# A causal convolution and two MLP layers on one core: staging of the weight split, order of the chains, and the crossing of block 0 changed

## The chip, the cores and the metric

One Trainium2 chip, one of its cores. The metric is the device time of one execution in microseconds; of several runs the median is given. Engines are named as the profile names them: PE (TensorE, the matmuls), PEld (its weight loads), DVE (VectorE), ACT (ScalarE), POOL (GpSimd), SP (SyncE, which here issues nearly all DMAs).

## The reference, cut to what matters

`x` is 2 x 4096 x 192, that is 8192 rows of 192 columns in fp32.

```
w   = softmax over the 7 taps of weight[8, 7]         # one set of taps for each group of 24 columns
x1  = causal convolution of x along the sequence with w
h   = x1 @ moe_w_in   (192 x 2048);  g = max(0.01 h, h);       x2  = g @ moe_w_out   (2048 x 192)
h   = x2 @ moe2_w_in  (192 x 2048);  g = h where h >= 1, 0 where h <= -1, else (h + 1)^2 / 4
out = g @ moe2_w_out  (2048 x 192)
```

## The kernel before, in words

The rows are cut into 16 blocks of 512. Columns lie on partitions. A block's layer is a **chain** of 8 **pairs**; a pair takes 256 of the 2048 hidden columns in two halves, e = 0 and 1. A pair's **up** (`add_up`, L594) makes two banks of hidden values from 18 matmuls, and its **down** (`add_down`, L657) adds them into the block's result. The pairs are numbered n = 0 to 255 in the order of the list `pairs` (L799 to L810), so U4 is the up of pair 4 and D4 its down. Since inputs and weights are fp32, each is split into a high part in the matmul's type (fp32r) and a low rest, and products high x high, high x low and low x high are added. The ups and the late downs use half the rows of the array for each of two matmuls that run side by side.

Pairs 0 to 15 (EARLY, L804) are layer one of blocks 0 and 1, interleaved; from then on a chain follows a chain in the order of `chains` (L805): before, block 2 of layer one (pairs 16 to 23), blocks 0 and 1 of layer two (24 to 39), block 3 of layer one (40 to 47), block 2 of layer two, and so on, alternating. A layer-two chain needs all 8 pieces of that layer's weights the first time; both layers' weights then stay on the chip. PE's order is `steps` (L812 to L817): U(n+2) stands ahead of D(n).

Between up and down a pair's values pass three engines. In layer one ACT applies the leaky function twice (`gh` and the bank itself, L625), and DVE subtracts (`gl`, L630). In layer two DVE clips (`s`, L638), ACT squares (L643), DVE takes the maximum (`g`, L647), ACT rounds it (`gh`, L650) and POOL subtracts (`gl`, L653).

**The weights** come in 32 pieces, 16 a layer, an in piece and an out piece for each p (`add_weights`, L229). The DRAM words are 8 bytes (`raw` has a low word and a high word). The steps of a piece: load by SP (L241 or L249); `lower` on ACT (L257) scales the high word into `ba`; `shift` on DVE (L261) moves its bits; `sign` on DVE (L264) sets the sign; `rest` on DVE (L270) scales the low word into `bp`; `total` on POOL (L274) adds both; `copy` on ACT (L285) makes the high part; `sub` on POOL (L290) the low part. `shift` and `sign` write a tile of their own, `wf`.

**The convolution** of a block (`add_conv`, L433 on): blocks 0 and 1 are transposed by PE (L486), take some of their taps on PE (L537, L542) and the others on DVE (L531); blocks 2 and up are transposed by DVE (L521) and have 12 taps on DVE. The result is split by `add_split` (ACT L406, then DVE or, for block 0, POOL, L410). The matmuls that take columns 64 to 127 and 0 to 63 from the other half of the partitions need `add_cross`: for block 0 two copies on ACT (L427) and two subtractions on DVE (L432), for all others two DMAs from the tile to itself (L420).

**The order of the work** is made on the host when the program is built. Every step is added to a `Plan` (L36) with its engine, a cost in ns, what it reads and writes, and, for PE's main steps, a due time. `Plan.order` (L79) computes the latest time of each step and then lists steps: an engine that is free takes the ready step with the earliest latest time. `COUNT` (L194) gives the buffers of each tile. On the chip each engine runs its list strictly in order.

Of the kernel before, what the change touches and what calls it, by code (L numbers as in the profile page):

```python
# [145 lines left out]
def kernel(  # L146
# [267 lines left out]
    def add_cross(dst, y=None):  # L414

        halves = (slice(0, DB), slice(DB, 128)), (slice(DB, 128), slice(0, DB))
        for to, of in halves:
            if y is None:
                plan.add(
                    dma, 300, lambda to=to, of=of: nc.sync.dma_start(  # L420
                        out=dst()[to, 2:4].bitcast(F32), in_=dst()[of, 0:2].bitcast(F32)
                    ),
                    reads=[(dst, 0), (dst, 1)], writes=[(dst, 2), (dst, 3)], uses=[dst],
                )
                continue
            plan.add(
                act, 610, lambda to=to, of=of: nc.scalar.copy(dst()[to, 2], y()[of]),  # L427
                reads=[y], writes=[(dst, 2)], uses=[dst],
            )
            plan.add(  # L430
                dve, 710,
                lambda to=to, of=of: nc.vector.tensor_tensor(  # L432
                    out=dst()[to, 3], in0=y()[of], in1=dst()[of, 0], op=ALU.subtract  # L433
                ),
                reads=[y, (dst, 0)], writes=[(dst, 3)], uses=[dst],
            )

    def add_conv(at, j):
# [33 lines left out]
        if early:  # L472
# [31 lines left out]
        else:  # L504
# [40 lines left out]
        for i in range(2):  # L545
            y = ys[i]
            if early and i:
                for k in range(NP):
# [4 lines left out]
            else:
# [314 lines left out]
```

## Time and profile before

| | |
|---|---|
| median of 3 runs | 1156.53 us (1156.28 to 1156.88) |
| the profiled execution, its own time | 1156.47 us |
| its span, first to last instruction | 1154.8 us |
| PE busy | 1137.4 us, 99% of the span |
| DVE busy | 865.3 us, 75% |
| ACT busy | 752.1 us, 65% |
| POOL busy | 421.6 us, 37% |
| TensorE clock granted, mean | 0.997 |

The page gives shares of the whole span. The program has three stages with different loads: the start up to pair 2, where blocks 0 and 1 are convolved and the first weights are made; the stretch in which weights are still being made; and the long rest with all weights there. So the windows and lines below are cut by stage. A busy PE is counted from a matmul's start to a modelled end, so short waits are seen better in the times between starts and in the waits that the timeline prints in brackets.

### The profile page before, as it was taken

How to read it: one execution, taken by the hardware profiler on the slowest of the kernel's cores; microseconds unless marked ns; L12 is line 12 of the kernel's file. 1: busy time of each engine (PE TensorE's matmuls, PEld its weight loads, DVE VectorE, ACT ScalarE, POOL GpSimd, SP SyncE). 2: the span in 40 equal slices, each digit the busy share in tenths (PEclk: the TensorE clock that was granted, in tenths of full speed). 3: DMA queues.
4: the chain of work that ended last, by engine and by line, in shares of the span. 5: the costliest groups of instructions: out<-in, count | busy, mean ns of one | idle time of the engine just before them, and what ended most of it. 6: DMA issues, size and time to landing. Idle time of an engine off the chain costs nothing.

```text
span 1154.8 us, 24741 instructions
## 1 busy us (share of the span) xinstructions
PE 1137.4 (99%) x9662; PEld 1081.5 (94%) x9662; DVE 865.3 (75%) x1278; ACT 752.1 (65%) x1320; POOL 421.6 (37%) x375
## 2 busy tenths in 40 slices
PE   8999979999999999999999999999999999999998
PEld 4778957888999999999999999999999999999998
DVE  7899989968678685877858678685867866474774
ACT  5767766656576675757667576665757666575764
POOL 4544587315051240604225061331605224060354
PEclk9999999999999999999999999999999999999999
DMA  4625122202002020110202002020210100000000
GB/s 129 158 71 143 56 60 51 52 1 56 15 19 52 19 47 6 39 32 19 51 8 50 15 20 51 20 49 4 46 25 20 33 20 20 15 20 15 20 12 17
DMA packets 124484, 44.87 MB, mean 39 GB/s; under 512 B 108624, under 2 KB 120400, under 8 KB 124368
## 3 DMA queue, kind: packets, MB, share of 16 engines
q1 hardware_dynamic: 123952, 43.08, 16.8%
q8 instruction: 75, 1.23, 0.4%
q14 instruction: 41, 0.34, 0.1%
q10 hardware_dynamic: 416, 0.23, 0.1%
HBM read 20.74 MB, written 6.29 MB: 23 GB/s over the span
## 4 chain that ended last, share of the span: by engine, by line
PE 95%; DVE 2%; issue 1%; ACT 1%; POOL 1%; DMA 1%; SPq 0%; ACTq 0%; DVEq 0%; POOLq 0%
PE bank L590 90%; PE bank L675 3%; PE bank L537 1%; DMA wraw<-in_x_dram 1%; DVE g L647 0%; DVE wf L261 0%; DVE s L638 0%; PE bank L763 0%; ACT s L643 0%; POOL wa L274 0%; DVE wp L270 0%; PE bank L542 0%; POOL gl L653 0%; PE bank L312 0%; ACT wa L257 0%
## 5 line engine op out<-in xcount | busy, mean ns | idle before, releaser
L590 PE MATMUL bank<-x,wi_h 64*128 64x512 f32 x3072 | 533.5, 388 | 4.1 <-ACT wi_h L285 2.7
L653 POOL TENSOR_TENSOR gl<-g,gh 128x512 fp32r<-128x512 f32 x256 | 339.6, 1347 | 497.5 <-ACT gh L650 491.7
L590 PEld LDWEIGHTS bank<-x,wi_h 64*128 64x128 f32 x3072 | 403.5, 184 | 21.2 <-issue 4.1
L590 PE MATMUL bank<-x,wi_l 64*128 64x512 f32 x1536 | 392.7, 387 | 2.1 <-POOL wi_l L290 2.1
L625 ACT ACTIVATE gh<-bank 128x512 fp32r<-128x512 f32 x246 | 146.4, 599 | 199.2 <-PE bank L590 194.4
L630 DVE TENSOR_TENSOR gl<-bank,gh 128x512 fp32r<-128x512 f32 x246 | 165.1, 681 | 147.8 <-PE bank L590 111.3
L590 PE MATMUL bank<-gh,wo_b 64*128 64x512 f32 x960 | 249.5, 388 | 1.9 <-POOL wo_b L290 1.9
L590 PE MATMUL bank<-gl,wo_b 64*128 64x512 f32 x960 | 249.5, 388 | 0.0
L590 PE MATMUL bank<-gh,wo_h 64*128 64x512 f32 x960 | 249.2, 387 | 0.0
L590 PE MATMUL bank<-gh,wo_l 64*128 64x512 f32 x960 | 249.0, 387 | 0.0
L590 PE MATMUL bank<-gl,wo_h 64*128 64x512 f32 x960 | 249.0, 387 | 0.0
L590 PEld LDWEIGHTS bank<-x,wi_l 64*128 64x128 f32 x1536 | 236.5, 184 | 8.5 <-POOL wi_l L290 3.0
L643 ACT ACTIVATE s<-s,half 128x512 f32<-128x512 f32 x256 | 173.4, 718 | 105.1 <-DVE s L638 103.6
L638 DVE TENSOR_SCALAR s<-bank 128x512 f32<-128x512 f32 x256 | 164.9, 684 | 83.0 <-PE bank L590 82.4
L647 DVE TENSOR_TENSOR g<-bank,s 128x512 f32<-128x512 f32 x256 | 168.5, 686 | 28.9 <-ACT s L643 22.9
L650 ACT CAST gh<-g 128x512 fp32r<-128x512 f32 x256 | 156.2, 619 | 43.4 <-DVE g L647 38.3
L590 PEld LDWEIGHTS bank<-gh,wo_b 64*128 64x128 f32 x960 | 152.1, 185 | 4.6 <-POOL wo_b L290 2.3
L590 PEld LDWEIGHTS bank<-gl,wo_b 64*128 64x128 f32 x960 | 151.7, 185 | 3.0 <-POOL gl L653 0.8
L590 PEld LDWEIGHTS bank<-gh,wo_h 64*128 64x128 f32 x960 | 152.0, 185 | 2.2
L590 PEld LDWEIGHTS bank<-gh,wo_l 64*128 64x128 f32 x960 | 151.9, 185 | 2.3
L590 PEld LDWEIGHTS bank<-gl,wo_h 64*128 64x128 f32 x960 | 151.8, 185 | 2.3
L531 DVE SCALAR_TENSOR_TENSOR xy<-xT,taps,xy 128x512 f32<-128x512 f32 x171 | 150.6, 911 | 0.6
(120 smaller groups left out, 790.2 us busy)
## 6 DMA issues: line engine op xcount, KB each, us to landing
x<-x SPq DMA_DIRECT2D x62, 256.0 KB, 3.6
xy<-in_x_dram SPq DMA_DIRECT2D x112, 64.0 KB, 2.5
wraw<-in_moe_w_in_dram SPq DMA_DIRECT2D x32, 192.0 KB, 3.4
wraw<-in_moe_w_out_dram SPq DMA_DIRECT2D x16, 384.0 KB, 3.2
out_dram<-o SPq DMA_DIRECT2D x90, 64.0 KB, 1.9
wraw<-in_x_dram SPq DMA_DIRECT2D x2, 384.0 KB, 6.1
out_dram<-s SPq DMA_DIRECT2D x1, 192.0 KB, 2.0
out_dram<-s ACTq DMA_DIRECT2D x1, 192.0 KB, 2.0
```

The costliest lines, as they stand in the source:

```text
L531: nc.vector.scalar_tensor_tensor(out=ys[i](), in0=t()[:, i, k:k + T], scalar=taps[:, i, k:k + 1], in1=ys[i](), op0=ALU.mult, op1=ALU.add,)
L537: nc.tensor.matmul(out=ys[1](), lhsT=flat(k), rhs=t()[:, 1, 2 * k:2 * k + T], start=(k == 0), stop=(k == NP - 1))
L590: nc.tensor.matmul(out=out_(), lhsT=w[e][r], rhs=v[e][r], start=start and i == 0, stop=stop and i == len(todo) - 1)
L625: lambda dst=dst, h=h: nc.scalar.activation(out=dst(), in_=h(), func=ACTF.Prelu, alpha=0.01),
L630: lambda a=a, b=b, h=h: nc.vector.tensor_tensor(out=b(), in0=h(), in1=a(), op=ALU.subtract),
L638: lambda s=s, h=h: nc.vector.tensor_scalar(s(), h(), 1.0, -1.0, ALU.min, ALU.max),
L643: lambda s=s: nc.scalar.activation(out=s(), in_=s(), func=ACTF.Square, scale=0.5, bias=half),
L647: dve, 680, lambda s=s, g=g, h=h: nc.vector.tensor_tensor(out=g(), in0=h(), in1=s(), op=ALU.max),
L650: plan.add(act, 620, lambda a=a, g=g: nc.scalar.copy(a(), g()), reads=[g], writes=[a])
L653: lambda a=a, b=b, g=g: nc.gpsimd.tensor_tensor(out=b(), in0=g(), in1=a(), op=ALU.subtract),
L675: nc.tensor.matmul(out=out_[part](), lhsT=w, rhs=v, start=start and i == 0, stop=stop and i == len(todo) - 1)
```

## The change

Four parts. (1) `wf` is gone: `shift` and `sign` work in place in `ba`, of which there are four (`wa=4`, two before), and `wp` has three. (2) `rest` runs on POOL instead of DVE, 32 times. (3) The chains go block 2 of layer one, blocks 0, 1 **and 2** of layer two, blocks 3 and 4 of layer one, and from there alternating as before; the loads of x for blocks 3 and up are not planned before the up of a pair 16 pairs earlier. (4) Block 0 is crossed by two DMAs as the others are. Besides, the convolutions of blocks 0 and 1 are added at steps of their own (`C0`, `C1`), so that four of PE's taps for block 1 stand in one run in PE's list, and the planner's costs are set anew.

```
-    COUNT = dict(wraw=4, wf=2, wa=2, wp=2, xy=4, ...)
+    LEAD = 16
+    COUNT = dict(wraw=4, wa=4, wp=3, xy=4, ...)
...
+        bits = lambda: ba().bitcast(U32)
         def shift():
-            nc.vector.tensor_scalar(bf(), ba().bitcast(U32), 3, None, ALU.logical_shift_left)
+            nc.vector.tensor_scalar(bits(), bits(), 3, None, ALU.logical_shift_left)
         def sign():
             nc.vector.scalar_tensor_tensor(
-                out=bf(), in0=raw()[:, :, 1], scalar=0x80000000, in1=bf(), op0=ALU.bitwise_and, op1=ALU.bitwise_or
+                out=bits(), in0=raw()[:, :, 1], scalar=0x80000000, in1=bits(), op0=ALU.bitwise_and, op1=ALU.bitwise_or
             )
         def rest():
-            nc.vector.tensor_scalar(bp(), raw()[:, :, 0], 2.0 ** -29, None, ALU.mult)
+            nc.gpsimd.tensor_scalar(bp(), raw()[:, :, 0], 2.0 ** -29, None, ALU.mult)
...
-        plan.add(act, 550, lower, reads=[raw], writes=[ba])
-        plan.add(dve, 430, rest, reads=[raw], writes=[bp])
-        plan.add(dve, 400, shift, reads=[ba], writes=[bf])
-        plan.add(dve, 600, sign, reads=[raw, bf], writes=[bf])
-        plan.add(pool, 1220, total, reads=[bf, bp], writes=[ba])
+        plan.add(act, 555, lower, reads=[raw], writes=[ba])
+        plan.add(pool, 800, rest, reads=[raw], writes=[bp])
+        plan.add(dve, 470, shift, reads=[ba], writes=[ba])
+        plan.add(dve, 715, sign, reads=[raw, ba], writes=[ba], chain=ba)
+        plan.add(pool, 1110, total, reads=[ba, bp], writes=[ba], chain=ba)
...
             if i == 0:
-                add_cross(dst, None if j else y)
+                add_cross(dst)
...
-                plan.add(dma, 2300, lambda i=i: load(i), reads=["under way"], writes=[raws[i]])
+                plan.add(dma, 2300, lambda i=i: load(i), reads=[("under way", at // 2 - LEAD)] if at // 2 > LEAD else ["under way"], writes=[raws[i]])
...
-    chains = [(0, 2), (1, 0), (1, 1)]
-    for j in range(3, NB):
+    chains = [(0, 2), (1, 0), (1, 1), (1, 2), (0, 3)]
+    for j in range(4, NB):
         chains += [(0, j), (1, j - 1)]
...
-    steps = ["U0", "U1", "D0"]
+    steps = ["C0", "U0", "U1", "C1", "D0"]
```

What it moves, at three places. On POOL, around the first `gl` of pair 24, the first pair of layer two (`wp` is the scaled low word, `wa` the whole word, the names with 85, 89 and 91 are layer two's split weights). Before:

```order
L274 TENSOR_TENSOR wa<-wf,wp 128x384
L460 COPY xT<-xT 128x2x6
L290 TENSOR_TENSOR wo_l_89<-wa,wo_h_87 128x256
L290 TENSOR_TENSOR wo_b_91<-wa,wo_b_91 128x2x64
L653 TENSOR_TENSOR gl<-g,gh 128x512 x2
L274 TENSOR_TENSOR wa<-wf,wp 128x384
L653 TENSOR_TENSOR gl<-g,gh 128x512 x2
L290 TENSOR_TENSOR wi_l_85<-wa,wi_h_83 128x384
```

After:

```order
L292 TENSOR_TENSOR wi_l_85<-wa,wi_h_83 128x384
L272 TENSOR_SCALAR wp<-wraw 128x384 x2
L292 TENSOR_TENSOR wo_b_91<-wa,wo_b_91 128x2x64
L642 TENSOR_TENSOR gl<-g,gh 128x512 x2
L276 TENSOR_TENSOR wa<-wa,wp 128x384
L292 TENSOR_TENSOR wo_l_89<-wa,wo_h_87 128x256
L642 TENSOR_TENSOR gl<-g,gh 128x512 x2
L292 TENSOR_TENSOR wi_l_85<-wa,wi_h_83 128x384
```

Ahead of the first `gl` stand before 24 totals, 12 `wi_l`, 12 `wo_l` and 12 `wo_b`; after, 32 scalings, 29 totals, 15 `wi_l`, 13 `wo_l` and 14 `wo_b`. So all scalings, and all but the end of the last three pieces, now come before layer two.

On DVE, from the last maximum of pair 28 to the first of pair 30 (`s` clips, `g` maxima of layer two, `wp`, `wf` weight steps). Before:

```order
L647 TENSOR_TENSOR g<-bank_65,s 128x512
L638 TENSOR_SCALAR s<-bank_66 128x512
L638 TENSOR_SCALAR s<-bank_67 128x512
L270 TENSOR_SCALAR wp<-wraw 128x384 x2
L261 TENSOR_SCALAR wf<-wa 128x384 x2
L264 SCALAR_TENSOR_TENSOR wf<-wraw,wf 128x384
L647 TENSOR_TENSOR g<-bank_66,s 128x512
L647 TENSOR_TENSOR g<-bank_67,s 128x512
L638 TENSOR_SCALAR s<-bank_64 128x512
L638 TENSOR_SCALAR s<-bank_65 128x512
L264 SCALAR_TENSOR_TENSOR wf<-wraw,wf 128x384
L647 TENSOR_TENSOR g<-bank_64,s 128x512
```

After:

```order
L636 TENSOR_TENSOR g<-bank_65,s 128x512
L627 TENSOR_SCALAR s<-bank_66 128x512
L627 TENSOR_SCALAR s<-bank_67 128x512
L412 TENSOR_TENSOR x<-yz,x 128x512
L636 TENSOR_TENSOR g<-bank_66,s 128x512
L636 TENSOR_TENSOR g<-bank_67,s 128x512
L510 STREAM_TRANSPOSE xT<-xy 128x512
L627 TENSOR_SCALAR s<-bank_64 128x512
L627 TENSOR_SCALAR s<-bank_65 128x512
L510 STREAM_TRANSPOSE xT<-xy 128x512
L636 TENSOR_TENSOR g<-bank_64,s 128x512
```

The weight steps have left this place. From the end of pair 15's values to the end of pair 31's there are 117 DVE instructions before (14 `wp`, 15 + 14 `wf`, 12 taps, 3 transposes) and 86 after (none of `wp`, 12 shifts, 13 signs, 2 taps, 2 transposes); the clips, maxima and subtractions of the pairs are the same 48 but for one clip.

On SP, early in the program, with block 0's crossing (`x<-x`). Before:

```order
L249 DMA wraw<-in_moe_w_in_dram 64x3x256 x2
L241 DMA wraw<-in_moe_w_out_dram 128x2x384
L249 DMA wraw<-in_moe_w_in_dram 64x3x256 x2
L241 DMA wraw<-in_moe_w_out_dram 128x2x384
L249 DMA wraw<-in_moe_w_in_dram 64x3x256 x2
L420 DMA x<-x 64x1024 x2
```

After:

```order
L251 DMA wraw<-in_moe_w_in_dram 64x3x256 x2
L243 DMA wraw<-in_moe_w_out_dram 128x2x384
L421 DMA x<-x 64x1024 x2
L251 DMA wraw<-in_moe_w_in_dram 64x3x256 x2
L243 DMA wraw<-in_moe_w_out_dram 128x2x384
L251 DMA wraw<-in_moe_w_in_dram 64x3x256 x2
L421 DMA x<-x 64x1024 x2
```

The first `x<-x` after is block 0's, ahead of the loads of pieces p = 2; the second, like the only one before, is block 1's.

## Rows read from the trace of the kernel before

**Rows 1.** The page: busy us, share of the span, instructions.

```profile
PE 1137.4 (99%) x9662; PEld 1081.5 (94%) x9662; DVE 865.3 (75%) x1278; ACT 752.1 (65%) x1320; POOL 421.6 (37%) x375
```

**Rows 2.** Windows: from:to, length, busy (count) of PE PEld DVE ACT POOL, PEclk, DMA.

```profile
102.78:150.57 47.79, 47.79 (x419) 46.59 (x419) 46.41 (x73) 36.72 (x72) 26.30 (x26) 1.00 0.28 79
150.57:185.36 34.79, 26.64 (x189) 19.44 (x188) 31.35 (x46) 22.00 (x42) 30.03 (x28) 0.90 0.26 58
185.36:1147.00 961.64, 961.64 (x8483) 944.98 (x8479) 699.84 (x1009) 622.99 (x1061) 316.45 (x251) 1.00 0.13 27
94.40:177.53 83.13, 76.90 (x624) 67.73 (x622) 77.47 (x118) 58.82 (x115) 53.88 (x53) 0.98 0.28 75
```

**Rows 3.** Timeline of PE, 144 to 170 us: start, length, and wait before.

```profile
144.78 0.48 PE L590 MATMUL bank<-gh,wo_b 64*128 64x512 f32 x2
...
149.09 0.47 PE L590 MATMUL bank<-gh,wo_b 64*128 64x512 f32 x2
...
159.00 0.73 PE L590 MATMUL bank<-x,wi_h 64*128 64x512 f32 x4 [2.02 <-ACT wi_h L285]
...
169.09 0.50 PE L590 MATMUL bank<-x,wi_l 64*128 64x512 f32 x2 [1.49 <-POOL wi_l L290]
```

**Rows 4.** Lines of DVE, 94.45 to 177.5 us: count, busy us, mean ns, idle before.

```profile
L270 DVE TENSOR_SCALAR wp<-wraw 128x384 uint32<-128x384 uint32 x14 | 11.7, 856 | 0.0
L638 DVE TENSOR_SCALAR s<-bank 128x512 f32<-128x512 f32 x17 | 11.1, 681 | 1.2 <-PE bank L590 1.1
L531 DVE SCALAR_TENSOR_TENSOR xy<-xT,taps,xy 128x512 f32<-128x512 f32 x12 | 10.7, 890 | 0.1
L264 DVE SCALAR_TENSOR_TENSOR wf<-wraw,wf 128x384 uint32<-128x384 uint32 x15 | 8.5, 581 | 0.2
L261 DVE TENSOR_SCALAR wf<-wa 128x384 uint32<-128x384 uint32 x15 | 8.4, 576 | 1.2 <-ACT wa L257 1.1
L410 DVE TENSOR_TENSOR x<-yz,x 128x512 fp32r<-128x512 f32 x4 | 4.1, 1027 | 0.1
```

**Rows 5.** Lines of POOL, 5 to 200 us, same columns.

```profile
L274 POOL TENSOR_TENSOR wa<-wf,wp 128x384 uint32<-128x384 uint32 x32 | 35.5, 1111 | 57.2 <-DVE wf L264 41.4 <-DVE wp L270 8.7 <-ACT xy L527 6.5
L290 POOL TENSOR_TENSOR wi_l<-wa,wi_h 128x384 fp32r<-128x384 f32 x16 | 18.0, 1127 | 5.9 <-ACT wi_h L285 5.9
L290 POOL TENSOR_TENSOR wo_l<-wa,wo_h 128x256 fp32r<-128x256 f32 x16 | 13.8, 861 | 0.7 <-ACT wo_h L285 0.7
L290 POOL TENSOR_TENSOR wo_b<-wa,wo_b 128x128 fp32r<-128x128 f32 x16 | 8.8, 553 | 8.1 <-ACT wo_b L285 8.1
```

**Rows 6.** Timelines of POOL and of DVE, the first 26 us.

```profile
2.56 0.29 POOL masks.py:199 TENSOR_SCALAR_AFFINE_SELECT ident<-ident 128x128 f32<-128x128 f32 x1
...
15.47 1.27 POOL L410 TENSOR_TENSOR x<-xy,x 128x512 fp32r<-128x512 f32 x1 [2.08 <-ACT x L406]
17.96 1.18 POOL L274 TENSOR_TENSOR wa<-wf,wp 128x384 uint32<-128x384 uint32 x1 [1.22 <-DVE wf L264]
...
18.20 1.16 DVE L270 TENSOR_SCALAR wp<-wraw 128x384 uint32<-128x384 uint32 x1
...
25.27 0.36 DVE L270 TENSOR_SCALAR wp<-wraw 128x384 uint32<-128x384 uint32 x1
```

**Rows 7.** The chain that ended last, up to 60 us: start, length, what.

```profile
18.68 0.90 PE bank L590 x6
...
41.30 4.33 PE bank L590 x36
45.63 4.78 PE bank L675 x20
```

**Rows 8.** Block 1's crossing: SP's timeline, and line L420 to 130 us.

```profile
27.12 1.17 SPq L420 DMA_DIRECT2D x<-x  x2
...
DMA to landing us min/median/max: 3.1/4.0/4.7
```

**Rows 9.** Page, costliest groups: ACT's step on a layer-one pair's values.

```profile
L625 ACT ACTIVATE gh<-bank 128x512 fp32r<-128x512 f32 x246 | 146.4, 599 | 199.2 <-PE bank L590 194.4
```

More of the change, by code (lines that the diff above doesn't have):

```diff
@@ L294, in add_weights @@
         if o == 0:
-            copy(550, wi_h[m][:, g], ba)
-            sub(pool, 1280, wi_l[m][:, g], ba, wi_h[m][:, g])
+            copy(510, wi_h[m][:, g], ba)
+            sub(pool, 1130, wi_l[m][:, g], ba, wi_h[m][:, g])
         else:
@@ L300, in add_weights @@
             copy(300, wo_b[m][:, k, 0, :], lambda: v()[:, :, 128:D], 1)
-            sub(pool, 1020, wo_l[m][:, k, :], lambda: v()[:, :, 0:128], wo_h[m][:, k, :])
-            sub(pool, 670, wo_b[m][:, k, 1, :], lambda: v()[:, :, 128:D], wo_b[m][:, k, 0, :], 1)
+            sub(pool, 860, wo_l[m][:, k, :], lambda: v()[:, :, 0:128], wo_h[m][:, k, :])
+            sub(pool, 550, wo_b[m][:, k, 1, :], lambda: v()[:, :, 128:D], wo_b[m][:, k, 0, :], 1)
     def add_warm():
@@ L412, in add_split, with add_cross @@
         )
[L414 to L425, printed above, removed]
-            plan.add(
[L427 to L433, printed above, removed]
+    def add_cross(dst):
+        for to, of in (slice(0, DB), slice(DB, 128)), (slice(DB, 128), slice(0, DB)):
+            plan.add(
+                dma, 300,
+                lambda to=to, of=of: nc.sync.dma_start(
+                    out=dst()[to, 2:4].bitcast(F32), in_=dst()[of, 0:2].bitcast(F32)
                 ),
-                reads=[y, (dst, 0)], writes=[(dst, 3)], uses=[dst],
+                reads=[(dst, 0), (dst, 1)], writes=[(dst, 2), (dst, 3)], uses=[dst],
             )
@@ L475, in add_conv @@
             plan.add(
-                dma, 1000,
+                dma, 800 if j else 3400,
                 lambda: nc.sync.dma_start(out=v(), in_=x[b, s0:s0 + T, :].rearrange("(n p) c -> p n c", p=128)),
@@ L550, in add_conv @@
                         pe, 870, lambda k=k: tap_pair(k), reads=[("diagonal", k), (t, 1)], writes=[y],
-                        uses=[t, spare], chain=(y, "taps"),
+                        uses=[t, spare], chain="main" if j else (y, "taps"),
                     )
@@ L564, in add_conv @@
                     plan.add(
-                        dve, 780, lambda i=i, k=k: tap(i, k), reads=[(t, i), y], writes=[y], uses=[t],
+                        dve, 900, lambda i=i, k=k: tap(i, k), reads=[(t, i), y], writes=[y], uses=[t],
                         chain=(y, "taps"),
@@ L609, in add_up @@
                 pe, 3 * PASS, lambda c=c: up(c), reads=[(src, 2 * c), (src, 2 * c + 1), (("w", m, 0, p), 0)],
-                writes=[*hs] + (["under way"] if n == GO else []), uses=[src], due=main(3 * PASS), chain="main",
+                writes=[*hs] + [("under way", n)] + (["under way"] if n == GO else []), uses=[src], due=main(3 * PASS), chain="main",
             )
@@ L825 @@
             up, n = step[0] == "U", int(step[1:])
+            if step[0] == "C":
+                add_conv(2 * pairs.index((0, n, 0)) - AHEAD, n)
+                continue
             m, j, p = pairs[n]
-            if up and m == p == 0:
+            if up and m == p == 0 and j >= E0:
                 add_conv(2 * n - AHEAD, j)
```

8 lines of the change are left out of this document (4 added, 4 removed).

## The prediction

> **What bounds the kernel now.** I read the page first: PE is busy 99% of the span [rows 1], which alone says that only the remaining waits can go. Then the windows [rows 2]. From 185.36 us on PE is busy in all 961.64 us, so nothing there can be won by moving other engines' work. From 102.78 to 150.57 it is busy too. Between, from 150.57 to 185.36, it is busy for 26.64 of 34.79 us, and the granted clock is 0.90. That stretch is layer two of block 0, while the weights of layer two are still being made.
>
> Then PE's timeline, for the waits themselves [rows 3]. Without waits the same matmul of two pairs in a row starts at 144.78 and at 149.09, so a pair takes 4.31 us. The bracketed waits name POOL (`wi_l`) and ACT (`wi_h`): PE waits for weights. But the engine named is only the last in a row. Who is late is seen in the window from 94.40 to 177.53, which runs from the last DVE instruction on pair 15's values to the last on pair 31's: DVE is busy 77.47 of 83.13 us, while POOL is busy 53.88 and ACT 58.82 [rows 2]. Sixteen pairs need 16 x 4.31 = 69.0 us of PE; they took 83.1. So **DVE is the bound there, and costs PE 14.1 us**. Its lines say what it does [rows 4]: beside the pairs' own values, 14 scalings of low words at 0.856 us (11.7 us busy), 30 shifts and signs (16.9 us), and 12 convolution taps for block 3 (10.7 us).
>
> The second place is the start. The chain of waits has the first up at 18.68 us and U4 at 41.30 [rows 7]. From U4 on the chain is PE alone, 4.33 us for two ups and 4.78 us for two downs [rows 7], to the end of the first stage.
>
> **The change part by part.**
>
> *DVE from pair 16 to 31.* By the changed order it has 86 instructions where 117 were. At the measured means [rows 4]: 48 clips, maxima and subtractions x 0.681 = 32.7; 12 shifts x 0.576 = 6.9; 13 signs x 0.581 = 7.6; 2 taps x 0.890 = 1.8; 11 others at no more than 1.027 = 11.3. Sum 60.3 us against 69.0 us of PE: DVE now has 8.7 us to spare where it was 14.1 short. (A sum of means is an upper figure, since neighbouring records overlap at their ends: the 17 clips, 11.6 us by their mean, are 11.1 us busy [rows 4].) What went: the scalings (to POOL), ten taps (to the two later layer-two chains), and five weight steps (done earlier). So the wait of the stretch goes: **14.1 us**, less if DVE's order still makes PE wait (the first rival).
>
> *Where the moved taps stand.* By the changed order DVE has, in the three layer-two chains (pairs 24 to 47), 96 clips and maxima, 21 taps (block 3's and nine of block 4's), 6 weight steps and 20 others: 65.4 + 18.7 + 3.5 and 20 at 0.681 to 1.027, together 101.2 to 108.1 us by means, 4% less for the overlap: 97 to 104. PE takes 24 x 4.31 = 103.4. So the cover is thin here: DVE nearly sets the pace for 100 us, though it comes to the stretch with time to spare and may be a pair late before PE waits. Bounds 0 and 4 us of new waits; I take **0.5**, nearer the lower end, since the pairs that follow one layer-two chain ran without waits at a like density of taps (from 185.36 us on [rows 2]).
>
> *The scaling on POOL.* No row shows a GpSimd multiply of 128 x 384 32-bit words. From below: a one-input POOL operation on 128 x 128 took 0.29 us [rows 6], three times that is 0.87, an upper figure if part of 0.29 is fixed. From above: the two-input add on the same 128 x 384 takes 1.11 us [rows 5]. I take 0.8, and keep 0.3 and 1.1 as bounds from these rows; a slower conversion is the second rival. POOL then has, ahead of the first `gl` of layer two, 32 scalings x 0.8 + 29 totals x 1.111 + 15 `wi_l` x 1.127 + 13 `wo_l` x 0.861 + 14 `wo_b` x 0.553 = 25.6 + 32.2 + 16.9 + 11.2 + 7.7 = 93.6 us, plus some 4 us for block 0's low part (1.27 [rows 6]) and small copies: about 98. It can start at about 8 us, and the pairs of layer two begin at 102.78 + 6 x 4.31, some 128 us: 22 us to spare. In the first stage two downs and two ups take 9.1 us [rows 7], and a pair of pieces costs POOL 1.6 + 2.2 + 1.1 + 0.9 + 0.6 = 6.4. So POOL's added 25.6 us cost nothing at the end; the cover is the 22 us.
>
> *In-place shift and sign, more `wa` tiles.* Same instructions, no time of their own: the four tiles let a piece start before the last one's `sub` is through.
>
> *Block 0 crossed by DMA.* Two copies of ACT and two subtractions of DVE go; two DMAs come, issued by SP in 1.17 us, and they landed 3.1 to 4.7 us after their issue for block 1 [rows 8]. They wait for block 0's low part on POOL, which ended at 15.47 + 1.27 = 16.7 us before [rows 6]. After, the three DVE taps ahead of it start about 1 us sooner (the first piece's shift and sign now stand behind them), but those two (1.16) stand ahead of the add: 15.2 to 16.7. With 0.6 us to the second issue and 3.1 to 4.7 to land, U0's last third starts at 19.0 to 22.1; I take 20.1. SP queues the loads of p = 2 behind the crossing; they come 1.2 us later and are needed only by U2. The gain of the two ACT and two DVE steps is in this chain, not beside it.
>
> *From there to U4.* U0 ends at 20.1 + 0.8 = 20.9. On ACT stand `gh`, a `lower`, three more leaky steps, then block 1's high part: six at about 0.6 [rows 9], to 24.5; on DVE then block 1's low part and the first `gl`, 2 x 0.68: 25.8. U1 and the four taps of block 1 (now in one run) are done on PE by then. D0 is half of 2.4 us behind each of two `gl`: ends at 28.2. Then two ups 4.33 and two downs 4.78 [rows 7]: U4 at 37.3 instead of 41.30. Weights do not stop it: POOL, walked the same way, has p = 2's `wo_b` at 34.7 for D2 at 34.9. **Gain 4.0 us**, with 5.1 and 2.0 at the ends of the crossing, and 1 if POOL is a little later.
>
> *The clock.* PE now stands idle for about 2.5 us ahead of U0 and 2.3 us in it. Before, waits such as 2.02 and 1.49 us, 8.15 us in all, went with a granted clock of 0.90 over 34.79 us [rows 2, 3], that is 3.5 us lost. Half as much waiting in the start may cost half of it, 1.7, or nothing, as before; I take 0.8.
>
> **The sum**, against the profiled execution's own 1156.47 us (0.06 below the median; its span is 1.67 less): 1156.47 - 14.1 + 0.5 - 4.0 + 0.8 = **1139.7 us**.
>
> **The rivals.**
>
> *The stretch keeps part of its wait, by the port.* A DVE scaling took 0.36 us alone and 1.16 us beside a POOL add [rows 6], which itself took 1.18 instead of some 1.0; its mean was 0.856 [rows 4]. So DVE and POOL hold each other up, and 25.6 us more of POOL can hold DVE. If each of the 16 layer-two scalings holds a DVE step by its 0.8, that is 12.8 us against 8.7 to spare: 4.1 back. If DVE's idle time in the stretch (83.13 - 77.47 = 5.7 us [rows 2]) comes again, 9.8 back. So 1144 to 1149.5. Against it: the scalings that did the waiting are themselves gone from DVE, and clips, maxima and subtractions, which read a bank, stay at 0.68 beside a busy POOL. The Trainium skill, page "SBUF — State Buffer", section "Who interferes with whom", says that GpSimd shares a port pair with VectorE as an exclusive lock, so that one of the two fully blocks for a whole instruction. By that rule this rival is what moving work to GpSimd does; rows 6 agree with it.
>
> *POOL becomes the bound* (slower). POOL's place is ahead of the first `gl` of layer two. If a scaling takes r, POOL is late by 32 x (r - 0.8) - 22 us, and PE waits there instead. That eats the gain of 16.8 at r = 2.0 us; at 2.5 it is 1139.7 + 54.4 - 22 = 1172. For it: it multiplies whole numbers by a fraction and reads every second word, which no POOL row of before does. Against it: the add of two inputs is 1.11 on the same size [rows 5].
>
> *The order does not carry it:* the list is made by costs, and if block 0's crossing, loads and conversions come in another rhythm, start and stretch each keep most of their waits: 1150 to 1157.
>
> **How the numbers follow.** Forecast 0.76, port 0.16, POOL 0.05, order 0.03. A measurement of this kernel can tell about 0.2%, 2.3 us. Faster: all but POOL's and half of the last, 0.93; slower 0.05; the same 0.02. The range runs from the best start with no wait left, 1156.47 - 14.1 - 5.1 = 1137.3, rounded to 1137.0, into the port's rival to 1147.0.
>
> **What would show it.** Right: U4 at 36 to 39 us; no bracketed PE wait over 0.5 us from 100 us to the end; a granted clock of 1.00 from 40 us to 1130; DVE busy under 60 us over pairs 16 to 31; `rest` on POOL at 0.7 to 1.1 us. Wrong: PE waits on POOL `gl` or `wi_l` past 120 us, DVE shifts or taps over 1.0 us on the mean, or U0's last third after 22 us.

## The result, and the profile after

The changed kernel takes **1139.97 us** (median of 4 runs, 1139.70 to 1140.33), the kernel before 1156.70 beside it (median of 4): a ratio of 0.9852, 95% interval 0.9835 to 0.9869. Forecast were 1139.7 us, in a range of 1137.0 to 1147.0. The span of the profiled execution went from 1154.8 to 1138.3 us.

The page's first part, as [rows 1]:

```profile
PE 1130.9 (99%) x9662; PEld 950.2 (83%) x9662; DVE 862.9 (76%) x1244; ACT 752.1 (66%) x1318; POOL 466.2 (41%) x407
```

PE's share reads 99% before and after. What changed stands in the windows (columns as in [rows 2]):

```profile
100.51:1130.66 1030.15, 1030.15 (x9085) 879.13 (x9085) 780.89 (x1112) 681.57 (x1170) 385.39 (x310) 1.00 0.15 31
91.87:162.57 70.70, 70.70 (x602) 57.60 (x603) 56.00 (x88) 55.81 (x110) 65.56 (x63) 1.00 0.35 87
126.42:229.96 103.54, 103.54 (x914) 86.94 (x912) 98.09 (x142) 74.75 (x125) 77.50 (x65) 1.00 0.16 32
```

The first row begins at U18, the up of the third pair of block 2 in layer one, six pairs ahead of layer two: from there to the last down PE waits for nothing, at a granted clock of 1.00 (by the starts of its ups 0.3 us in all are lost there). The second row is the stretch from the last DVE step on pair 15 to the last on pair 31: 70.70 us, where it was 83.13 with DVE busy 77.47 of them [rows 2]. (It is cut at DVE's steps, so the 12.4 us between the two are not PE's gain; that is read from PE's own starts below.) DVE is now busy 56.00, and POOL, at 65.56 of 70.70, is the fuller engine. The third row is the three chains in a row (pairs 24 to 47): DVE is busy 95% of it, and PE still waits for nothing.

The chain that ended last, as [rows 7] (start, length, what):

```profile
36.41 2.56 PE bank L664 x10
38.97 4.33 PE bank L579 x36
43.30 4.78 PE bank L664 x20
...
100.51 1030.15 PE bank L579 x9084
```

U4 starts at 38.97 us instead of 41.30. By its first matmul, U18 starts at 100.44 instead of 102.71, and the last down of layer two at 1130.27 instead of 1146.62. So the 16.5 us of span split in two, but for 0.1 behind the last down: **2.3 us up to U18, and 14.1 us behind it** (1043.91 us from U18 to that last down before, 1029.83 after).

Steps of DVE and POOL, 5 to 200 us (line, count, busy us, mean ns, idle before), as [rows 5]; the first line is the taps, the others are weight steps. (The layers' weights lie in DRAM as 64-bit floats, not as fp32; these steps make one fp32 word of the two 32-bit halves.) In the kernel before, the same 5 to 200 us had 0.946 us on the mean for a tap, 0.701 for a sign and 0.495 for a shift; [rows 4] has a shorter window:

```profile
L520 DVE SCALAR_TENSOR_TENSOR xy<-xT,taps,xy 128x512 f32<-128x512 f32 x27 | 27.6, 1035 | 0.2
L266 DVE SCALAR_TENSOR_TENSOR wa<-wraw,wa 128x384 uint32<-128x384 uint32 x32 | 24.0, 753 | 0.8
L263 DVE TENSOR_SCALAR wa<-wa 128x384 uint32<-128x384 uint32 x32 | 20.2, 632 | 3.4 <-ACT wa L259 3.3
```

```profile
L272 POOL TENSOR_SCALAR wp<-wraw 128x384 uint32<-128x384 uint32 x32 | 41.4, 1295 | 8.6 <-DMA wraw<-in_moe_w_in_dram 5.7 <-DMA wraw<-in_moe_w_out_dram 0.5
L276 POOL TENSOR_TENSOR wa<-wa,wp 128x384 uint32<-128x384 uint32 x32 | 34.2, 1072 | 9.3 <-DVE wa L266 8.4
```

A scaling on POOL takes 1.295 us, not the 0.8 that was taken, and more than the add of two inputs on the same tile.

### The profile page after: what moved, and what is told of

It is laid out like the page before. It is cut to its first block, busy times and chain, and to the rows that moved or that the text cites. A ratio compares the mean times of both kernels' runs of the same rounds, so it can differ in the third digit from the quotient of the medians.

```text
span 1138.3 us, 24723 instructions
## 1 busy us (share of the span) xinstructions
PE 1130.9 (99%) x9662; PEld 950.2 (83%) x9662; DVE 862.9 (76%) x1244; ACT 752.1 (66%) x1318; POOL 466.2 (41%) x407
## 4 chain that ended last, share of the span: by engine, by line
PE 96%; POOL 1%; DVE 1%; DMA 1%; issue 0%; ACT 0%; SPq 0%; DVEq 0%; POOLq 0%; ACTq 0%
PE bank L579 93%; PE bank L664 3%; POOL wp L272 0%; DMA wraw<-in_moe_w_in_dram 0%; DMA raw_taps<-in_weight_dram 0%; POOL wa L276 0%; PE bank L752 0%; DVE wa L263 0%; DVE xy L520 0%; DVE x L389 0%; POOL wi_l L292 0%; POOL wo_b L292 0%; DVE xy L559 0%; DVE wa L266 0%; ACT wi_h L287 0%
## 5 line engine op out<-in xcount | busy, mean ns | idle before, releaser
L579 PE MATMUL bank<-x,wi_l 64*128 64x512 f32 x1536 | 441.5, 386 | 0.0
L579 PEld LDWEIGHTS bank<-x,wi_l 64*128 64x128 f32 x1536 | 264.4, 184 | 25.9
L579 PE MATMUL bank<-gh,wo_h 64*128 64x512 f32 x960 | 282.5, 386 | 0.0
L579 PE MATMUL bank<-gh,wo_b 64*128 64x512 f32 x960 | 282.5, 386 | 0.0
L579 PE MATMUL bank<-gh,wo_l 64*128 64x512 f32 x960 | 282.5, 386 | 0.0
L579 PE MATMUL bank<-gl,wo_b 64*128 64x512 f32 x960 | 282.5, 386 | 0.0
L579 PE MATMUL bank<-gl,wo_h 64*128 64x512 f32 x960 | 282.3, 386 | 0.0
L579 PEld LDWEIGHTS bank<-gh,wo_h 64*128 64x128 f32 x960 | 170.8, 184 | 16.1 <-DVE yz L685 0.3
L579 PEld LDWEIGHTS bank<-gl,wo_h 64*128 64x128 f32 x960 | 170.8, 184 | 15.9
L520 DVE SCALAR_TENSOR_TENSOR xy<-xT,taps,xy 128x512 f32<-128x512 f32 x171 | 171.8, 1022 | 0.6
```

Source lines behind the costliest of these rows:

```text
L520: nc.vector.scalar_tensor_tensor(out=ys[i](), in0=t()[:, i, k:k + T], scalar=taps[:, i, k:k + 1], in1=ys[i](), op0=ALU.mult, op1=ALU.add,)
L579: nc.tensor.matmul(out=out_(), lhsT=w[e][r], rhs=v[e][r], start=start and i == 0, stop=stop and i == len(todo) - 1)
```

## The experiments

Twelve kernels. The change has four parts: the **scaling** on POOL, the staging **tiles** (shift and sign in place, four `wa`, three `wp`), the three **chains** in a row, and the **crossing** of block 0 by DMA. The first four runs undo one part each in the changed kernel, three others make one part alone in the kernel before, and the rest vary one size or put single scalings back. The crossing alone was not run, and no run undoes what goes with the four parts by itself: the planner's other costs, the later loads of x, and the steps `C0` and `C1`. In the table, times are medians, the other columns are from one profiled execution each: U4 the start of its first matmul in us, "U18" that start against the changed kernel's 100.44 us, "behind" the time from U18 to the last down of layer two, over its 1029.83, and "ahead" how many of the 32 pieces POOL has started to add before it starts its first `gl` of layer two. The profiled execution of a_wa2 was the fastest of its eleven, 1155.35 us. One profile's start is good to some 0.6 us: U0 began between 16.67 and 17.30 us in the changed kernel and those that differ from it by one part or size (a_rest2 left out).

| Kernel | us | U4 | U18 | behind | ahead |
|---|---|---|---|---|---|
| before | 1156.5 | 41.23 | +2.3 | +14.1 | 24 |
| changed | 1140.0 | 38.90 | 0 | 0 | 29 |
| u_rest: scaling undone | 1142.8 | 38.49 | -0.5 | +2.4 | 29 |
| u_chains: chains undone | 1142.7 | 39.74 | +0.9 | +1.7 | 29 |
| u_cross: crossing undone | 1142.9 | 38.89 | +1.2 | +1.3 | 29 |
| u_tiles: tiles undone | 1159.3 | 42.75 | +3.8 | +16.5 | 25 |
| b_rest: scaling alone | 1156.7 | 39.98 | +1.0 | +15.5 | 25 |
| b_tiles: tiles alone | 1147.5 | 39.71 | +0.8 | +6.3 | 27 |
| b_chains: chains alone | 1160.4 | 41.62 | +2.7 | +16.3 | 24 |
| a_wa2: two `wa` tiles | 1158.1 | 41.70 | +2.7 | +12.6 | 25 |
| a_wp2: two `wp` tiles | 1143.4 | 41.14 | +2.4 | +1.4 | 29 |

### One part undone: u_rest, u_chains, u_cross, u_tiles

u_rest:

```diff
-            nc.gpsimd.tensor_scalar(bp(), raw()[:, :, 0], 2.0 ** -29, None, ALU.mult)
+            nc.vector.tensor_scalar(bp(), raw()[:, :, 0], 2.0 ** -29, None, ALU.mult)
-        plan.add(pool, 800, rest, reads=[raw], writes=[bp])
+        plan.add(dve, 430, rest, reads=[raw], writes=[bp])
```

> The changed kernel with the scaling of the low words back on DVE (its planner cost 430), all else as changed. Load theory (what DVE has to do from pair 16 to 31 against PE's 68.9 us decides): DVE gets 14 scalings back there but still has only 1 tap, by its means 68.8 us, and its worst lateness over any row of pairs is 5.3 us, where the kernel before had 19.1 us and lost 14.1: 0 to 1.5 us of waits, 1140 to 1142 us, most of it in the start. Rival 'the scaling alone is the cause': the 14 scalings are half of what left DVE there, so at least 7 us come back, 1147 us or more, with waits of PE between 130 and 180 us. Rival 'port': with less work on POOL, taps fall from 1.02 to about 0.95 us and shifts from 0.63 to 0.5.

Measured 1142.82 us (1141.92 to 1143.49), ratio 0.988 (0.9865 to 0.9895), 0.8 us over the load theory's range. The scaling is not the cause of the gain: with all 32 back on DVE, 13.6 of the 16.5 us stay. The price is 2.4 us behind U18, and PE has it in one place, between the starts of U34 and U35 at the end of layer two's first block. The timeline brackets 1.4 us of it as waits (start, length, and in brackets the wait before):

```profile
171.89 0.50 PE L579 MATMUL bank<-gh,wo_b 64*128 64x512 f32 x1 [0.25 <-ACT yz L683]
173.53 0.50 PE L579 MATMUL bank<-gh,wo_b 64*128 64x512 f32 x1 [1.14 <-DVE yz L685]
```

The port rival missed: taps stayed at 1.043 us (shifts fell to 0.526, signs rose to 0.903).

u_chains:

```diff
-    chains = [(0, 2), (1, 0), (1, 1), (1, 2), (0, 3)]
-    for j in range(4, NB):
+    chains = [(0, 2), (1, 0), (1, 1)]
+    for j in range(3, NB):
```

> The changed kernel with the old order of the chains of layer two (two in a row instead of three), all else as changed. Load theory: 9 taps of block 3 come back into pairs 16 to 31, 64.4 us of DVE by its means against 68.9 of PE, worst lateness 3.8 us: no wait, 1140 to 1141 us. Rival 'the order of the chains is the cause': the ten moved taps (10.7 of the 22.4 us that left DVE) bring back half of the gain or more, 1147 us or more, with waits of PE between 130 and 185 us.

Measured 1142.67 us (1141.75 to 1142.92), ratio 0.9877 (0.9861 to 0.9894): 1.7 us over the load theory's end and far from the rival's. The order of the chains isn't the cause either. The 1.7 us behind U18 are lost between 136 and 155 us, where PE's waits of 0.17 to 0.33 us (at 138, 146 and 151 us) name DVE. The nine taps that stand between U16 and U33 are not shown as their cause: two of them run at 122 and 123 us, and the other seven from 151 us on.

u_cross puts the two ACT copies and the two DVE subtractions of the kernel before back for block 0:

```diff
-                add_cross(dst)
+                add_cross(dst, None if j else y)
```

> The changed kernel with block 0 crossed by two ACT copies and two DVE subtractions again, all else as changed. Load theory for the stretch: nothing of it changes, no PE wait past 100 us. Start: the two DMAs land at 19.05 and 20.28 us in the changed kernel, and U4 starts at 38.97; with the two ACT and two DVE steps back, 2.6 us of those engines stand in the chain again, as in the kernel before (U4 at 41.30): U4 at 39.5 to 41.3, 1140.5 to 1142.3 us. Rival 'the start's gain is the two convolution runs and the order, not the crossing': U4 within 0.4 us of 38.97, 1139.6 to 1140.4 us.

Measured 1142.90 us (1142.74 to 1143.00), ratio 0.9881 (0.9867 to 0.9896): over both ranges. U4 starts at 38.89 us, as in the changed kernel: **the crossing by DMA gains nothing at the place where the prediction put its gain.** U2 even starts 0.7 us earlier (28.48 against 29.22), and then waits for POOL:

```profile
30.22 0.50 PE L592 MATMUL bank<-x,wi_l 64*128 64x512 f32 x2 [1.00 <-POOL wi_l L292]
```

The 2.9 us come later: 1.2 by U18, with two waits of 0.5 and 0.1 us in the first stage, at 74 and 75 us; 0.7 at U34, with a wait of 0.25 at 173; and 0.7 between 236 and 245 us. The list that the planner makes with these four steps in it is another one; what in it makes these waits was not followed up.

u_tiles has the old tiles, and shift and sign write another tile:

```diff
-    COUNT = dict(wraw=4, wa=4, wp=3, xy=4, xT=2, x=3, yz=3, g=2, s=2, gh=4, gl=4, o=1)
+    COUNT = dict(wraw=4, wf=2, wa=2, wp=2, xy=4, xT=2, x=3, yz=3, g=2, s=2, gh=4, gl=4, o=1)
...
-            nc.vector.tensor_scalar(bits(), bits(), 3, None, ALU.logical_shift_left)
+            nc.vector.tensor_scalar(bf(), bits(), 3, None, ALU.logical_shift_left)
```

> The changed kernel with the old staging tiles (two for the words, two for the bits, two for the rest; shift and sign write another tile), all else as changed. Load theory with a lead: a piece then waits for the subtraction of the piece before the last, so fewer weight steps are done ahead of the layer-two chain; DVE has 64.7 us by its means in pairs 16 to 31 but 111.8 in pairs 23 to 47 against 103.4 of PE, worst lateness 11.0 us (26 to 42), of which some 5 were free in the kernel before: 4 to 7 us of waits between 130 and 210 us, 1144 to 1147 us. Rival 'tiles cost nothing, the load of pairs 16 to 31 alone decides': 1140 to 1141 us.

Measured **1159.34 us** (1157.17 to 1161.73), ratio 1.0026 (1.0016 to 1.0035): slower than the kernel before, and 12 us over the higher of the two expectations. Three parts of the change together, without the tiles, are worth less than nothing. PE's waits (line, waited for, total, times, longest) name another engine than before:

```profile
PE bank L579 <- POOL gl L642: 4.2, 2, 2.7
PE bank L579 <- POOL wo_b L292: 2.8, 1, 2.8
PE bank L664 <- POOL wo_b L292: 1.5, 1, 1.5
PE bank L579 <- POOL wi_l L292: 1.2, 1, 1.2
```

The window from 150 to 190 us, of the kernel before, of u_tiles and then of the changed kernel:

```profile
150.00:190.00 40.00, 31.85 (x236) 23.84 (x234) 36.56 (x54) 25.83 (x48) 33.47 (x30) 0.91 0.23 50
```

```profile
150.00:190.00 40.00, 31.26 (x209) 23.40 (x207) 34.23 (x46) 20.93 (x39) 39.16 (x35) 0.83 0.24 46
```

```profile
150.00:190.00 40.00, 40.00 (x353) 33.27 (x351) 38.87 (x56) 27.71 (x47) 28.71 (x25) 1.00 0.15 23
```

POOL is busy 39.16 of 40 us and is the bound. The theory counted DVE's load alone; it fell here. In its place: **how far the conversion of the weights runs ahead of layer two decides, and the tiles set that.** The table's last two columns say it over all its kernels: with 24 or 25 pieces ahead they lose 12.6 to 16.5 us behind U18, with 27 they lose 6.3, with 29 at most 2.4. (a_rest2, below, is the exception, with 29 ahead and 13.7 lost: there POOL's work itself is made longer.) POOL's groups up to 131 us, shortly before it starts its first `gl` of layer two (at 131.4 to 137.1 us), count the pieces that have come to the add (of 32). u_tiles, then b_tiles (below), then the changed kernel:

```profile
L276 POOL TENSOR_TENSOR wa<-wf,wp 128x384 uint32<-128x384 uint32 x25 | 26.4, 1064 | 24.4 <-DVE wf L266 23.4 <-ACT xT L487 0.6
```

```profile
L275 POOL TENSOR_TENSOR wa<-wa,wp 128x384 uint32<-128x384 uint32 x27 | 29.3, 1084 | 43.1 <-DVE wp L271 29.4 <-DVE wa L265 13.6
```

```profile
L276 POOL TENSOR_TENSOR wa<-wa,wp 128x384 uint32<-128x384 uint32 x29 | 30.7, 1062 | 9.3 <-DVE wa L266 8.4
```

The kernel before has 24. What is missing at 131 us is done in the same 60 us in which POOL has the `gl` of layer two.

### One part alone: b_rest, b_tiles, b_chains

b_rest makes only u_rest's edit the other way round, in the kernel before.

> The kernel before with the scaling of the low words on POOL alone (planner cost 800), old staging tiles, old chains, old crossing. POOL theory, formed on the run with the old tiles (there POOL was busy 39.2 of the 40 us from 150 to 190, PE waited for its gl, wo_b and wi_l, and the run came out 2.8 us slower than before): with two tiles of each kind POOL can't work ahead in the first stage, its scalings fall into the stretch of layer two, and POOL takes DVE's place as the bound: 1156 to 1165 us, PE's waits there name POOL, POOL busy over 18.5 of 20 us from 150 to 170 and from 170 to 190. DVE-load theory, as it stood before the runs: DVE falls from 82.5 to 72.2 us in pairs 16 to 31, worst lateness 8.9 us, some 5 of them free: 1145 to 1148 us.

Measured 1156.69 us (1156.07 to 1157.04), ratio 0.9996 (0.9987 to 1.0006): no difference. In the window from 150 to 190 us DVE falls to 31.98 us of work (36.56 in the kernel before) and POOL rises to 36.71 (33.47), 18.67 of it up to 170 us and 18.04 behind, where the POOL theory wanted over 18.5 in both:

```profile
150.00:190.00 40.00, 31.10 (x229) 23.17 (x227) 31.98 (x46) 25.04 (x47) 36.71 (x32) 0.91 0.18 37
```

PE waits 4.2 us for POOL's `gl`, for which it did not wait before, 2.8 for its `wo_b` of layer two, and 0.7 for DVE (1.4 before); the loss is about the same (15.5 us behind U18, 14.1 before). So POOL stood right behind DVE in the kernel before, and to relieve DVE alone wins nothing.

b_tiles makes only the tiles' edit.

> The kernel before with the four staging tiles, the shift and sign in place and three tiles for the rest alone; scaling on DVE, old chains, old crossing. Load theory (DVE): some weight steps are done earlier, DVE has 78.2 us in pairs 16 to 31 (82.5 before) and its worst lateness is 12.6 us (19.1 before, which cost 14.1): 6 to 8 us of waits stay, for DVE: 1148 to 1151 us. Rival 'tiles help only POOL's lead': DVE stays the bound by itself and at most 2 us go, 1154 to 1157 us.

Measured **1147.49 us** (1146.24 to 1148.84), ratio 0.9922 (0.9905 to 0.9938): 8.8 us, over half of the whole gain, with the scaling still on DVE, and 0.5 us under the load theory's range. One wait of some size is left, and it names DVE, as that theory has it (beside it stand waits for POOL of 0.2 to 0.3 us and a granted clock of 0.91 from 170 to 190 us). But from 150 to 170 us, where PE is idle for 2.8 of 20 us, POOL is as full as DVE (19.98 and 19.97 us), so the run doesn't tell the two apart:

```profile
PE bank L591 <- DVE g L648: 2.3, 1, 2.3
```

```profile
150.00:170.00 20.00, 17.19 (x143) 12.92 (x141) 19.97 (x26) 12.59 (x24) 19.98 (x17) 1.00 0.11 27
```

The other 7.7 us of the gain belong to no part alone: scaling, chains and crossing win nothing or were not run alone in the kernel before, and each brings 2.7 to 2.9 us in the changed one.

b_chains makes only the chains' edit.

> The kernel before with three chains of layer two in a row alone. Load theory (DVE): 82.5 us in pairs 16 to 31 as before, but with block 4's taps the lateness runs on to 22.7 us (19.1 before): 14 to 18 us of waits, 1156 to 1160 us. Rival 'the order of the chains is what gains': taps go out of the stretch, at least 5 us are won, 1151 us or less.

Measured 1160.35 us (1158.75 to 1164.60), ratio 1.0037 (1.0025 to 1.0049): slower, just past the upper end that the load theory gave. The same edit that is worth 2.7 us in the changed kernel (u_chains) costs 4.1 here. The load theory's reason, that DVE is late already when block 4's taps come, fits the 16.3 us behind U18 (14.1 before), of which 2.9 are lost from 250 to 262 us; no run tests it apart.

### Sizes: a_wa2, a_wp2, a_rest2

a_wa2 keeps shift and sign in place and takes two of the four `wa` tiles away:

```diff
-    COUNT = dict(wraw=4, wa=4, wp=3, xy=4, xT=2, x=3, yz=3, g=2, s=2, gh=4, gl=4, o=1)
+    COUNT = dict(wraw=4, wa=2, wp=3, xy=4, xT=2, x=3, yz=3, g=2, s=2, gh=4, gl=4, o=1)
```

> The changed kernel with two wa tiles instead of four, still in place, three wp tiles. Lead theory (POOL, and with it all of a piece's steps, can work ahead only as far as wa tiles are free, and a wa tile is held until the last subtraction of its piece): by the changed order POOL has done 28 of the 32 scalings ahead of the first gl of layer two (all 32 in the changed kernel, 27 with the old tiles), so most of the 19.4 us that the old tiles cost comes back: 1150 to 1159 us, with POOL busy over 18.5 of 20 us from 150 to 170. Rival 'in-place alone, or the third wp tile, is what counts': 1140 to 1143 us.

Measured 1158.07 us (1155.35 to 1158.83), ratio 1.0001 (0.9992 to 1.0010), in the lead theory's range. By the ratios that is 17.2 of the 20.1 us that the old tiles cost (18.1 of 19.4 by the medians): **the number of `wa` tiles is most of what the tiles are worth, and without it the rest of the change gains nothing.** Four of them without the work in place were not tried. A `wa` tile is held from ACT's `lower` to POOL's last subtraction. With two, from the 7th to the 20th piece, a `lower` starts every 5.7 to 5.8 us (kernel before, b_rest, u_tiles and a_wa2); with four every 3.4 us (b_tiles, u_rest and the changed kernel), though each piece then takes longer to get through (14.0 to 14.7 us on the mean from its `lower` to its last subtraction against 8.4 to 8.8). The window, as above:

```profile
150.00:190.00 40.00, 31.28 (x243) 22.03 (x242) 37.01 (x52) 24.82 (x46) 37.83 (x35) 1.00 0.21 39
```

a_wp2 takes one of the three `wp` tiles away.

> The changed kernel with two wp tiles instead of three. Lead theory: wp is held from the scaling to the add, both on POOL, so two are enough: 31 scalings ahead of the first gl of layer two, worst lateness of DVE 3.3 us: 1139.5 to 1142 us. Rival 'the third wp tile carries the lead': 1146 us or more.

Measured 1143.41 us (1142.73 to 1143.78), ratio 0.988 (0.9866 to 0.9893): over the lead theory's range, under the rival's. 2.4 of the 3.4 us are lost by U18, in the start, where POOL brings p = 2's `wo_b` late:

```profile
38.65 0.50 PE L664 MATMUL bank<-g,wo_b 128*128 128x512 f32 x1 [1.84 <-POOL wo_b L292]
```

a_rest2 issues each scaling on POOL twice into the same tile:

```diff
             nc.gpsimd.tensor_scalar(bp(), raw()[:, :, 0], 2.0 ** -29, None, ALU.mult)
+            nc.gpsimd.tensor_scalar(bp(), raw()[:, :, 0], 2.0 ** -29, None, ALU.mult)
```

> The changed kernel with each scaling on POOL done twice into the same tile, which computes nothing else: its cost goes from 1.3 to 2.6 us a piece, and the program's order stays. Prediction's sum for POOL as the bound: 32 x (2.6 - 0.8) - 22 us spare = 35.6 us late ahead of the first gl of layer two; by what was measured, some 112 us of POOL's work plus 41.4 more in the about 123 us from 8 to 131 us: 30 to 36 us late. So 1170 to 1178 us, with PE waiting for POOL in the first stage (wo_b, wi_l) and again between 120 and 190 us. Rival 'POOL has plenty of room, its rate doesn't count': under 1145 us.

Measured 1173.66 us (1173.55 to 1174.07), ratio 1.0148 (1.0133 to 1.0163). POOL's groups over the whole run:

```profile
L272 POOL TENSOR_SCALAR wp<-wraw 128x384 uint32<-128x384 uint32 x32 | 41.1, 1285 | 8.5 <-DMA wraw<-in_moe_w_in_dram 6.1
L273 POOL TENSOR_SCALAR wp<-wraw 128x384 uint32<-128x384 uint32 x32 | 39.6, 1238 | 2.6
```

39.6 us more of POOL cost 33.7 us, 5.9 less than was added, inside the range that was expected. The prediction's own formula for this rival gives 22 - 32 x (1.295 - 0.8) = 6.2 us to spare at the measured price. That the two are so close is not proof: not all of the 33.7 is a wait for POOL. From 8 us to its first `gl` of layer two, now at 165.6 us and not at 133.5, POOL was busy 143.04 of 157.6 us (108.23 of 125.5 in the changed kernel), so it stood idle nearly as long as there, and the granted clock was 0.95 over that stretch (1.00 there). U18 starts 19.9 us late, and 13.7 are lost behind it, under PE waits that name DVE and ACT as often as POOL:

```profile
PE bank L580 <- DVE yz L686: 4.5, 1, 4.5
PE bank L580 <- DVE gl L620: 3.2, 4, 2.0
PE bank L580 <- ACT wi_h L288: 3.2, 2, 1.7
PE bank L665 <- POOL wo_b L293: 2.6, 1, 2.6
```

Only POOL's work was added. The engine named by a wait is the last link, as in [rows 3].

### A version that might be faster: a_early1, a_early2

u_rest's U4 was 0.4 us earlier than the changed kernel's. These two leave the first scalings on DVE and the others on POOL (a_early2 with `g < 2`):

```diff
+        early = m == 0 and g < 1
-        plan.add(pool, 800, rest, reads=[raw], writes=[bp])
+        plan.add(dve if early else pool, 430 if early else 800, rest, reads=[raw], writes=[bp])
```

> The changed kernel with the scaling of the first piece of each of the first layer's two weights (p = 0) on DVE, all others on POOL. With all scalings on DVE the start was 0.4 us shorter (U4 at 38.49 us against 38.90, since the first up's last third and the second ups came earlier); here DVE's stretch in layer two stays as in the changed kernel (58.0 us by its means against 68.9 of PE): U4 at 38.3 to 38.9, no waits past 100 us, 1139.3 to 1140.0 us. Rival 'any other start makes its own waits' (with the old crossing two came in the first stage, and one in layer two): 1140.5 to 1142 us.

> The same with the scalings of p = 0 and p = 1 (four pieces) on DVE. U4 at 38.2 to 38.9 us, DVE 58.8 us by its means in pairs 16 to 31 as in the changed kernel, no waits past 100 us: 1139.2 to 1140.0 us. Rival as for one piece: 1140.5 to 1142 us.

Measured 1144.75 us (1143.65 to 1145.34) and 1141.48 (1141.46 to 1141.51): both slower than the changed kernel; the rival had the second, and the first came out over both ranges. Behind U18 a_early2 loses 0.1 us, as expected, but its U4 is at 39.94: PE waits 1.01 us for DVE's low part of block 0 and 1.01 for POOL's `wi_l`. a_early1 has U4 at 39.36, 0.5 us of waits in the first stage between 67 and 77 us, where u_cross has them too, and loses 2.3 us behind U18. The 0.4 us were within what one start differs from the next. No version tried beats the changed kernel.

## Why the prediction was right, and where its reasons were not

Forecast and measurement lie 0.3 us apart, and that is partly luck: the start gave 1.7 us less than was taken, and two terms that were added, 0.5 and 0.8, were not there.

**The stretch of layer two, 14.1 us.** Right in size: 14.1 measured. DVE was to be busy 60.3 us by means, an upper figure; it was 56.00. But the shares that the text gave were wrong. It put the wait's going down to the scalings (first), the ten taps and five weight steps done earlier. By the runs the scaling alone gives nothing, the chains alone cost 4.1 us, and what the text dismissed, "In-place shift and sign, more `wa` tiles: same instructions, no time of their own", gives 8.8 alone; undone, it takes 19 to 20 away. **This is the step that failed.** With it went the reading of DVE as the bound by itself: in b_rest DVE was relieved and POOL held PE as long. The sum held all the same, since DVE's 86 instructions were counted in the order of the finished change, and that order already had the tiles' lead in it. A sum over the order says how long an engine works; it doesn't say which edit put the order there.

**The scaling's price, 0.8 us.** It was 1.295, outside both the bounds (0.3 to 1.1) and the check (0.7 to 1.1). The lower neighbour row (0.29 us on 128 x 128) misled, and so did the upper: this one-input operation is slower than the two-input add (1.072). The cover carried it, but by the prediction's formula 6 us of it were left, not 22. The rival of POOL as the bound was nearer than its 0.05 said. PE's waits for a full POOL came in u_tiles and b_rest, there for want of tiles and not by the price, and a_rest2 came within 2 us of its formula (1139.7 + 35.6 = 1175.3 at 2.6 us, 1173.7 measured; see there for what that is worth).

**The residual over the three chains, 0.5 us.** Not there: DVE was busy 98.09 us of 103.54, near the lower end of the 97 to 104 that were worked out, and PE waited for nothing.

**The crossing.** Its own step was right: SP issued at 15.9 us, it landed after 3.1 to 3.8 us, and U0's last third started at 19.9 us on one half of the array's rows and at 20.3 on the other (20.1 taken).

```profile
DMA to landing us min/median/max: 3.1/3.5/3.8
```

**The walk to U4, 4.0 us.** It was 2.3. Two rows of PE's timeline show the mis-sized term:

```profile
19.32 0.50 PE L579 MATMUL bank<-x,wi_h 64*128 64x512 f32 x2 [1.24 <-DVE x L412]
23.27 3.70 PE L526 MATMUL bank<-xT,x 128*128 128x512 f32 x8
```

The four taps of block 1 were to be done beside U1, by 25.8 us, with DVE's `gl` the last to come. They are eight matmuls that start 0.43 us apart, and from U1's end at 23.3 they hold D0 until 26.4; D0 ends at 29.2 instead of 28.2. From there to U4 it took 9.7 us where 9.1 were taken, 0.3 of the difference a wait for POOL's `wo_b`. And the text's cause is wrong here too: the start's gain doesn't come from the crossing (u_cross has the same U4). It isn't pinned to another part either. In the changed kernel it goes with the tiles: undone, or with fewer, U4 is at 41.1 to 42.8. But in the kernel before the tiles alone have U4 1.5 us earlier, and the scaling alone, with the old tiles, 1.2 us.

**The clock, 0.8 us.** Not there. PE waited 1.24 us in U0, where 2.3 were supposed, and the granted clock is 1.00 in the windows above, in that of the first 40 us and in that from 40 to 1130.

**The port rival** (0.16). Its mechanism is there, its price isn't. POOL's timeline (start, length, wait before), then DVE's over the same time:

```profile
10.52 1.57 POOL L272 TENSOR_SCALAR wp<-wraw 128x384 uint32<-128x384 uint32 x1 [0.54 <-DMA wraw<-in_moe_w_out_dram]
12.24 1.21 POOL L272 TENSOR_SCALAR wp<-wraw 128x384 uint32<-128x384 uint32 x1 [0.15 <-DMA wraw<-in_moe_w_in_dram]
13.53 1.00 POOL L276 TENSOR_TENSOR wa<-wa,wp 128x384 uint32<-128x384 uint32 x1
14.53 1.35 POOL L412 TENSOR_TENSOR x<-xy,x 128x512 fp32r<-128x512 f32 x1
```

```profile
11.89 0.41 DVE L263 TENSOR_SCALAR wa<-wa 128x384 uint32<-128x384 uint32 x1
12.34 0.86 DVE L266 SCALAR_TENSOR_TENSOR wa<-wraw,wa 128x384 uint32<-128x384 uint32 x1
13.12 0.68 DVE L559 TENSOR_TENSOR xy<-bank,xy 128x512 f32<-128x512 f32 x1
13.73 1.03 DVE L263 TENSOR_SCALAR wa<-wa 128x384 uint32<-128x384 uint32 x1
14.79 1.51 DVE L266 SCALAR_TENSOR_TENSOR wa<-wraw,wa 128x384 uint32<-128x384 uint32 x1
```

The shift that began at 11.89, as a scaling ended on POOL, took 0.41 us; the one at 13.73, beside POOL's add, took 1.03. The sign took 0.86 us beside a scaling and 1.51 beside POOL's subtraction from 14.53 on, and the step with a bank input stays at 0.68. The Trainium skill, page "SBUF — State Buffer", section "Who interferes with whom", has the rule of the shared port pair as an exclusive lock; these rows agree, in the start. In these rows the longest steps stand beside POOL's adds and subtractions, which the kernel before has too, and not beside its scalings. In the stretch of layer two, where the rival put 4 to 10 us, shifts had 0.59 and signs 0.71 us on the mean (0.58 and 0.58 before [rows 4]), and DVE had the room. The check "taps over 1.0 us on the mean" was hit (1.035) and meant nothing: in u_rest, without any scaling on POOL, they had 1.043.

## What to carry to other kernels

Where several engines prepare data for one that must not wait, look at the number of staging tiles: here it set how much of the preparation was done before the stretch that needs the same engines for other work, and it was worth more than the work moved. Moving work from a full engine to an emptier one gained nothing where it landed in the same stretch: look at the receiver's busy time in that window, not over the span (POOL was busy 37% of the span before [rows 1], and 36.71 of the 40 us that mattered in b_rest). Price every edit apart, one alone and one undone: here the same edit of the chains is worth 2.7 us in one company and costs 4.1 in the other.

## What was not expected of the hardware

POOL's scaling of 128 x 384 words, with one input, took 1.295 us on the mean in the changed kernel, 1.318 in b_rest, and 1.285 and 1.238 in a_rest2, where the second reads what the first has just read; its add of two inputs took 1.072, 1.118 and 1.042. The Trainium skill, page "GPSIMD Engine Reference", section "Engine selection", has elementwise work of two inputs there about twice as slow as on VectorE and one-input work at roughly line rate; for these words the rows don't agree, the work of one input was the slower. What makes the scaling slow (the whole numbers, the fraction, or that it reads every second word) was not tried.

What waits of the same sum cost in clock differs, and not by kernel alone. From 150 to 190 us PE was busy 31.26 us in u_tiles and 31.28 in a_wa2, but did 209 matmuls in the one and 243 in the other: the granted clock was 0.83, a mean between its two levels, and 1.00. Those 34 matmuls are 3.9 us at 4.31 us for the 38 of a pair, and behind U18 u_tiles lost 3.9 us more than a_wa2. In u_tiles the waits came as 2.7, 1.5, 0.4, 1.2 and 2.8 us, in a_wa2 as eleven of at most 1.8. Whether that made the difference isn't shown: of a_wa2's eleven executions seven had a mean granted clock of 0.994 to 0.996 and took 1156.66 to 1158.83 us, and the profiled one, at 1.000 and 1155.35 us, is the fastest.
